# Twelve chunks of windowed attention and a two-layer network on one core: both halves of layer 1 by Strassen from the seventh chunk on, layer 2 in two banks, LayerNorm's squares on ScalarE

## The chip, the core and the metric

The kernel runs on one core of a Trainium2 chip. The core has five engines that run side by side, each through its own list of instructions in order: TensorE (PE; matrix products into the eight banks of PSUM; loads of its weights are listed as PEld), VectorE (DVE), ScalarE (ACT), GpSimd (POOL) and SyncE (SP; it issues DMAs). They wait for each other by semaphores. The metric is the time of one execution on the device in microseconds (us), as the median over runs.

## What is computed

Attention of 4 batches, 8 heads, 768 tokens, head size 64, over a window of 128 tokens and 4 sink tokens; then LayerNorm and a two-layer network of 512, 2048 and 512, and a residual:

```python
scores = scale * np.matmul(q, k.transpose(0, 1, 3, 2))
is_sink = pos[None, :] < n_sink                   # 4
in_window = (rel >= 0) & (rel < window)           # 128
a = softmax(np.where(is_sink | in_window, scores, -1e9))
x = np.matmul(a, v)                               # heads side by side: 4 x 768 x 512
xn = (x - mean(x)) / np.sqrt(var(x) + 1e-06) * g_ln
out = x + np.maximum(xn @ w_ch1, 0.0) @ w_ch2
```

Inputs and output are float32. Inside, operands of matrix products are bfloat16 and sums are float32.

## The kernel before

The 3072 tokens are cut into 24 tiles of 128 (t) and 12 chunks of 256 (c = 0 to 11, three to a batch; R = c % 3). A chunk goes through these steps, named by the operations in the program:

- **Loads.** GpSimd's queue loads q and k (`nat`, 128 KB a tile) and v (`vn`), casting to bfloat16. From chunk 4 on SyncE's queue transposes q and k by DMA into `kq` (`trq`, `trk`). Chunks 0 to 3 are transposed on TensorE (L672 for chunks 1 to 3, from `n4a`, `n4b`, `n4c`).
- **Attention.** `sc` (L754, L802): scores on TensorE into a pair of PSUM banks; `ex` (L758, L814): exponentials on ScalarE; `mk` (L826; a quarter of it on GpSimd, L821): masks on VectorE; `sv` (L721) and `av` (L854): values on TensorE, with the sum of the weights as a 65th column of every head.
- **LayerNorm.** On VectorE `rc` (reciprocal, L868), `x` (L870), `bn` (BN_STATS, L874) and `ag` (L876); on GpSimd `rs` (L882, L883: 1/sqrt of the variance); on VectorE `xc` (L885: centred and scaled). From chunk 2 on SyncE's queue transposes `xc` into `xnt` by DMA (L569), two transposes a chunk.
- **Layer 1.** Plain units `ph` (L1027): 8 matmuls of 256 columns into one bank, clipped into the hidden tile `hq` by ScalarE or VectorE (`rl`, L1037, L1039). From chunk 4 on the first half of the hidden columns (`hq[0]`) is made by Strassen's seven products `m1` to `m7` (L958, 8 matmuls of 128 columns each), with token sums `xt` on GpSimd (L938) and weight sums made once on VectorE (`wsum`, L923). Three product banks z, w, y are used; `tz` (L969) are copies of a bank to SBUF on ScalarE, after which the next product adds to the same bank; the sums `c11`, `c12`, `c22` are VectorE additions of a bank and a copy (L980) followed by a clip on ScalarE (L983); `c21` is clipped from its bank (L1001). The other half stays with four units.
- **Layer 2.** From chunk 2 on seven products `p1` to `p7` (Winograd's form, L1109, 8 matmuls of 256 columns each) with VectorE's operand sums `s1` to `s4` (L1092), the keeping sums `tm` (L1123: bank plus x) and the final sums `o` (L1130); the order is p1, p2, p7, p6, p4, p5, p3 in three banks x, y, w. SyncE's queue stores the result (L1154, L1159).

The order of all this is not that of the text. `Plan.op` only records operations with their engines, reads, writes and a priority; `Plan.run` then simulates the engines with a table of costs, gives each operation an engine, a start and its buffers out of the rings (`nat`, `kq`, `hq`, `tz`, the PSUM banks `one` and `pair`), and the operations are emitted in the order of these starts. Into TensorE's gaps of that simulated time before 24 us the last loop of the program lays matmuls on a tile of zeros (`junk`, L1236).

## Time and profile before

| what | value |
|---|---|
| time, median of 3 runs | 208.83 us (208.38 to 208.92) |
| span of the profiled execution | 206.6 us; it is an execution of its own, and its whole time is not listed apart |
| ScalarE, GpSimd busy, 140 to 155 us | 9.22 and 8.46 of 15 us |
| software DMA queue (GpSimd's) | 13.37 MB, 81.7% of 16 engines' span |
| hardware DMA queue (SyncE's) | 13.43 MB, 34.1% |
| median time from issue to landing, k, q, v | 4.6, 4.9, 6.9 us |

The span runs from the first to the last instruction; the time also holds what lies before and after it. A busy time adds up an engine's instructions, and two that overlap are counted twice. In the chain of waits each piece is followed back from the last instruction to what released it, so that its shares say what the end hangs on.

### The profile page before, as it was taken

What the parts mean: (1) busy time and instruction counts of PE and PEld (TensorE: products, weight loads), DVE (VectorE), ACT (ScalarE), POOL (GpSimd) and SP (SyncE); (2) the same over time, 40 slices, a digit from 0 to 9 for tenths busy, and PEclk for the clock granted to TensorE, in tenths of its full rate; (3) what the DMA queues carried; (4) which work ended last, traced back from release to release, by engine and by line L of the source; (5) the groups of instructions that cost most, each with busy time, mean ns of one, the idle gap of its engine ahead of it and who ended that gap; (6) DMA issues with size and microseconds to landing.
All of it is one profiled execution on the core that took longest, in us unless ns stands there. A gap on an engine that the chain in (4) does not pass through costs nothing.

```text
span 206.6 us, 6790 instructions
## 1 busy us (share of the span) xinstructions
PE 199.4 (97%) x2766; PEld 165.6 (80%) x2766; DVE 179.6 (87%) x437; ACT 119.7 (58%) x187; POOL 118.7 (57%) x170
## 2 busy tenths in 40 slices
PE   6888999999999999999999999999999999999994
PEld 2557996674698897898998988988988988988993
DVE  7589769899599899899989989989989989998693
ACT  3649477839555655666486486485486585560620
POOL 7977475279039029959649949968627229125000
PEclk9999999999999999999999999999999999999999
DMA  5999999999999999999999999899976411210302
GB/s 117 146 195 195 197 181 205 199 158 171 186 200 124 124 191 101 121 174 101 175 152 137 113 159 143 109 171 114 194 117 101 128 33 23 106 32 19 108 27 84
DMA packets 101341, 27.55 MB, mean 133 GB/s; under 512 B 89652, under 2 KB 99128, under 8 KB 101304
## 3 DMA queue, kind: packets, MB, share of 16 engines
q0 software_dynamic: 67712, 13.37, 81.7%
q1 hardware_dynamic: 33304, 13.43, 34.1%
q8 instruction: 22, 0.36, 0.7%
q10 hardware_dynamic: 288, 0.26, 0.4%
q14 instruction: 15, 0.12, 0.2%
HBM read 27.31 MB, written 6.29 MB: 163 GB/s over the span
## 4 chain that ended last, share of the span: by engine, by line
PE 90%; DMA 3%; DVE 3%; POOL 2%; issue 0%; DVEq 0%
PE one L1109 31%; PE one L1027 20%; PE one L958 12%; PE one L1058 7%; PE one L1020 7%; PE pair L854 5%; PE pair L802 4%; DMA n4b<-in_q_dram 3%; PE one L672 1%; PE pair L721 1%; POOL nat L626 1%; PE one L714 1%; DVE xnt L907 1%; DVE kq L595 1%; POOL vn L589 0%; DVE st L874 0%
## 5 line engine op out<-in xcount | busy, mean ns | idle before, releaser
L1027 PE MATMUL one<-xnt,w 128*128 128x256 bf16 x384 | 46.8, 273 | 0.0
L814 ACT ACTIVATE pe<-pair 128x1024 bf16<-128x1024 f32 (+1 forms) x40 | 36.3, 963 | 18.2 <-PE pair L802 18.2
L1037 ACT ACTIVATE hq<-one 128x512 bf16<-128x512 f32 x58 | 33.4, 590 | 17.9 <-PE one L1020 9.4
L1027 PEld LDWEIGHTS <-w 128*128 128x128 bf16 x384 | 36.3, 98 | 4.0
L1109 PEld LDWEIGHTS <-hs 128*128 128x128 bf16 x320 | 31.0, 98 | 4.0
L882 POOL TENSOR_SCALAR st<-st 128x1 f32<-128x1 f32 x24 | 6.4, 266 | 44.4 <-DVE rec L868 27.5
L826 DVE TENSOR_TENSOR pe<-pe,mask 128x1024 bf16<-128x1024 bf16 (+1 forms) x35 | 27.1, 799 | 1.6 <-ACT pe L814 1.4
L969 ACT COPY tz<-one 128x512 f32<-128x512 f32 x24 | 13.9, 585 | 20.6 <-PE one L958 19.2
L1109 PEld LDWEIGHTS <-hq 128*128 128x128 bf16 x240 | 22.2, 98 | 4.1 <-issue 0.5
L589 POOL DMA_DIRECT2D vn<-in_v_dram x24 | 21.9, 922 | 2.2 <-DMA w<-in_moe_w_ch_dram 1.2
L983 ACT ACTIVATE hq<-hq 128x512 bf16<-128x512 bf16 x24 | 15.1, 630 | 13.1 <-DVE hq L980 12.6
L1109 PE MATMUL one<-w,hq 128*128 128x256 bf16 x160 | 19.2, 273 | 0.0
L980 DVE TENSOR_TENSOR hq<-one,tz 128x512 bf16<-128x512 f32 x24 | 16.4, 684 | 1.9 <-PE one L958 1.0
L1130 DVE TENSOR_TENSOR ot<-one,tm 128x256 f32<-128x256 f32 x40 | 15.9, 412 | 2.1 <-PE one L1109 1.8
L1123 DVE TENSOR_TENSOR tm<-one,x 128x256 f32<-128x256 f32 x40 | 16.6, 414 | 1.2 <-PE one L1109 1.1
L870 DVE TENSOR_TENSOR x<-pair,rec 128x512 bf16<-128x512 f32 x24 | 16.6, 691 | 0.8
L874 DVE BATCH_NORM_STATS2 st<-x 128x6 f32<-128x512 bf16 x24 | 16.5, 687 | 0.2
L1020 PE MATMUL one<-xnt,w 128*128 128x128 bf16 x256 | 16.0, 219 | 0.5 <-DVE xnt L907 0.5
L687 POOL DMA_DIRECT2D nat<-in_q_dram x16 | 14.2, 893 | 3.7 <-DMA w<-in_moe_w_ch_dram 3.7
L938 POOL TENSOR_TENSOR xt<-xnt 128x256 bf16<-128x256 bf16 x16 | 12.2, 778 | 7.1 <-DMA xnt<-xc 7.0
L687 POOL DMA_DIRECT2D nat<-in_k_dram x16 | 14.8, 928 | 2.4 <-DMA w<-in_moe_w_ch_dram 2.4
L1020 PEld LDWEIGHTS <-w 128*128 128x128 bf16 x256 | 14.6, 98 | 1.6 <-issue 0.8
(130 smaller groups left out, 387.7 us busy)
## 6 DMA issues: line engine op xcount, KB each, us to landing
out_dram<-ot SPq DMA_DIRECT2D x17, 256.0 KB
w<-in_moe_w_ch_dram POOLq DMA_DIRECT2D x8, 512.0 KB, 12.8
vn<-in_v_dram POOLq DMA_DIRECT2D x24, 128.0 KB, 6.9
nat<-in_k_dram POOLq DMA_DIRECT2D x17, 128.0 KB, 4.6
nat<-in_q_dram POOLq DMA_DIRECT2D x17, 128.0 KB, 4.9
out_dram<-ot SPq DMA_DIRECT2D x14, 128.0 KB
kq<-nat SPq DMA_TRANSPOSE x32
xnt<-xc SPq DMA_TRANSPOSE x20
```

The costliest lines, as they stand in the source:

```text
L589: loads[b * RB + r, "v"] = P.op(f"vld{t}", {"POOL": (0.87, 0.9)}, prio, lambda e: G.dma_start(bv.t[:, :, 0:64], v[b, :, 128 * r:128 * (r + ...
L687: lambda e, nat=nat, ap=ap: G.dma_start(nat.t, ap), writes=[nat], dma=SW if c < 6 else (*SW[:2], PAR["llag"]), after=behind(c, 0 if soon e ...
L814: P.op(f"ex{c}{hp}", {"ACT": act(2 * n)}, d + 0.1 + 0.05 * j, lambda e, pp=pp, pb=pb: nc.scalar.activation(pb.t[:, :, 0:n], pp.t[:, :, 0:n ...
L826: V.tensor_mul(pb.t[:, :, 0:n], pb.t[:, :, 0:n], mm),
L870: P.op(f"x{t}", {"DVE": dve(512)}, d + xo + 0.11, lambda e: V.tensor_tensor(x.t.rearrange("p (a h c) -> p a h c", a=2, c=64), pv()[:, :, : ...
L874: P.op(f"bn{t}", {"DVE": fix(0.60)}, d + xo + 0.12, lambda e: V.bn_stats(st.t[:, 8:14], x.t), reads=[x], writes=[st, mv])
L958: nc.tensor.matmul(b.t[:, 128 * h:128 * h + 128], lhsT=lt[:, kk, 128 * h:128 * h + 128], rhs=rh[:, kk, :], start=first and h == 0 and kk = ...
L1020: nc.tensor.matmul(ph.t[:, 128 * s:128 * s + 128], lhsT=w1[u // 2][:, j, 128 * s:128 * s + 128], rhs=xnt.t[:, j, 128 * (u % 2):128 * (u % ...
L1027: nc.tensor.matmul(ph.t[:, 256 * s:256 * s + 256], lhsT=w1[ht // 4][:, j, 128 * (ht % 4):128 * (ht % 4 + 1)], rhs=xnt.t[:, j, :], start=j ...
L1037: nc.scalar.activation(hg.t[:, u % 4, :], ph.t, AF.Relu)
L1109: nc.tensor.matmul(at(r), lhsT=get(left, g)[:, v, s, :], rhs=rhs, start=first and n == 0, stop=n == 7, skip_group_check=True)
L1123: return P.op(f"tm{name}_{c}", {"DVE": dve(256, 1.14)}, pr - PAR["kp"], lambda e: V.tensor_tensor(tm[name].t, at(r), xs[i].t[:, sl], op=AL ...
```

## The change

In words:

- The simulated planner goes. `SCHEDULE` is a table with an engine and a start for each of the 1159 operations, `SLOTS` one with the buffer of each; `run` reads them. The order of chunks 0 to 3 stays as it was, apart from the fills on `junk`, which follow the table's gaps.
- The ring `one` has, beside its four banks, the four halves of the `pair` banks; `tz` has three tiles in place of two.
- From chunk 6 (`new=6`) `both()` makes both halves of the hidden columns by Strassen: 14 half products and no units. The sums are one VectorE instruction each that adds and clips (`TENSOR_ADD_SAT`). From chunk 7 the copy of m1 goes from bank to bank (`sd`, ScalarE), m2 adds to it, and c11 is a clip. A second set of weight sums (`wsumb`) is made on VectorE in chunks 4 to 6.
- From chunk 6 layer 2 goes p1, p2, p6, p7, p5, p4, p3 and alternates between two banks.
- From chunk 7 (`lnc=7`) `x` is made by an instruction that also sums the row, followed by a small scaling (`nm`); the squares are summed by ScalarE (`sq`); `rs` has a third step; `xc` is made by VectorE or ScalarE; the token sums by VectorE or GpSimd. The values lie 128 columns apart in the bank instead of 65.

The core of the diff:

```diff
+    def run(self):
+        engines = dict(P="PE", A="ACT", V="DVE", G="POOL", S="SP")
+        table = SCHEDULE.split()
+        assert len(table) == len(self.ops)
+        for o, entry in zip(self.ops, table):
+            o.eng, o.start = engines[entry[0]], int(entry[1:]) / 100
...
+        return sorted(self.ops, key=lambda o: (o.start, o.seq))
...
-    P.ring("one", [Slot(ones[i], f"one{i}", [banks[4 + i]]) for i in range(4)])
+    P.ring("one", [Slot(ones[i], f"one{i}", [banks[4 + i]]) for i in range(4)]
+           + [Slot(pairs[i][:, j, :], f"half{i}{j}", [banks[2 * i + j]], 1, True) for i in range(2) for j in range(2)])
...
-    ring("tz", 2, [128, 512], FP32)
+    ring("tz", 3, [128, 512], FP32)
...
+            P.op(f"x{t}", {"DVE": fix(0.62)}, d + xo + 0.11, lambda e: V.tensor_tensor_reduce(
+                out=x.t.rearrange("p (h c) -> p h c", c=64), in0=pv()[:, :, 0:64],
+                in1=rc().unsqueeze(2).to_broadcast([128, 8, 64]), scale=1.0, scalar=0.0, op0=ALU.mult, op1=ALU.add,
+                accum_out=st.t[:, 13:14]), reads=[po, rcb], writes=[x, st])
+            nm = Buf(f"nm{t}")
+            P.op(f"nm{t}", {"DVE": fix(0.07)}, d + xo + 0.12, lambda e: V.tensor_scalar_mul(
+                st.t[:, 12:13], st.t[:, 13:14], -1.0 / DM), reads=[st, x], writes=[nm])
+            P.op(f"sq{t}", {"ACT": (0.78, 0.9)}, d + xo + 0.13, lambda e: nc.scalar.activation(
+                xc.t, x.t, AF.Square, bias=st.t[:, 12:13], accum_out=st.t[:, 15:16]), reads=[x, st, nm], writes=[mv, xc])
...
+            G.tensor_tensor(st.t[:, 16:17], st.t[:, 17:18], mhalf, op=ALU.pow),
+            *([G.tensor_tensor(st.t[:, 8:9], st.t[:, 16:17], st.t[:, 12:13], op=ALU.mult)] if on_act else [])),
...
+            P.op(f"xc{t}", {"DVE": fix(0.33), "ACT": act(512)}, d + xo + 0.6, lambda e: V.tensor_scalar(
+                xc.t, x.t, st.t[:, 12:13], st.t[:, 16:17], op0=ALU.add, op1=ALU.mult) if e == "DVE" else nc.scalar.activation(
+                xc.t, x.t, AF.Identity, bias=st.t[:, 8:9], scale=st.t[:, 16:17]), reads=[x, st, mv, rs], rw=[xc])
...
+    def both(c, T, g, hq, tokens):
...
+        def total(n, bank, done, tz, pr):
+            outs[n] = Buf(f"{n}_{c}{g}")
+            o = P.op(f"c{n}_{c}{g}", {"DVE": dve(512, 1.14)}, pr, lambda e: V._custom_dve(
+                dve_ops.TENSOR_ADD_SAT, out=block(n), in0=banks_[bank].t.rearrange("p (i t) -> p i t", i=4),
+                in1=tz.t.rearrange("p (i t) -> p i t", i=4), s0=FMAX, s1=0.0),
+                reads=[done, tz], hold=[banks_[bank], hq], writes=[outs[n]])
+            return o
...
+        m1 = product(1, "z", "a11", "b11", True, second[:1])
+        if seeds:
+            seed = Buf(f"sd{c}{g}")
+            o1 = P.op(f"sd_{c}{g}", {"ACT": act(512)}, T + pos[0] - PAR["tzp"], lambda e: nc.scalar.copy(banks_["w"].t, banks_["z"].t),
+                      reads=[m1], hold=[banks_["z"]], writes=[banks_["w"], seed])
+        else:
+            t1, o1 = snap(1, "z", m1)
+        m5 = product(5, "y", 0, "t0", True)
+        t5, o5 = snap(5, "y", m5)
+        m2 = product(2, "w", "a12", "b21", not seeds, [o1] if seeds else [])
...
+        m6 = product(6, "z", 1, "t1", False, [o1])
+        t2, o2 = snap(6, "z", m6)
+        m3 = product(3, "y", 3, "b22", False, [o5])
+        total("c12", "y", m3, t2, T + pos[5] - late_)
+        m7 = product(7, "z", 2, "t2", False, [o2])
+        o3 = total("c22", "z", m7, t5, T + pos[6] - late_)
+        m4 = product(4, "z", "a22", "t3", False, [o3])
...
-        quick = halves(c, T, hq[0]) if strassen else None
-        for u in range(4 if strassen else 0, NH1 // 2):
+        tokens = token_sums(c, T) if strassen else None
+        quick = ([both(c, T, g, hq[g], tokens) for g in range(2)] if c >= PAR["new"] else [halves(c, T, hq[0], tokens)] if strassen else [])
+        for u in range(4 * len(quick), NH1 // 2):
...
+            bank = {n: Buf(f"bk{n}{c}", "one", full=True) for n in "xy"}
+            reg = {"z": ("x", 0), "l2": ("y", 256), "l1": ("y", 0), "r1": ("x", 256)}
```

What the table moves, at the three places that matter below.

TensorE between the last scores of tile 1 (`pair_62<-kq_85`) and chunk 1's transposes (`n4b`), before and then changed:

```order
L742 LDWEIGHTS ident
L742 MATMUL pair_62<-neg,ident 128x512
...
L754 LDWEIGHTS kq_85
L754 MATMUL pair_62<-kq_85 128x128
...
L672 LDWEIGHTS n4b_68
L672 MATMUL one_64<-ident,n4b_68 64x2x64
```

```order
L741 LDWEIGHTS kq_85
L741 MATMUL pair_62<-kq_85 128x128
...
L1351 LDWEIGHTS junk
L1351 MATMUL one_65<-junk 128x512
...
L1351 LDWEIGHTS junk
L1351 MATMUL one_65<-junk 128x128
...
L658 LDWEIGHTS n4b_68
L658 MATMUL one_64<-ident,n4b_68 64x2x64
```

Eight matmuls on the tile of zeros, six of 512 columns and two of 128, now stand ahead of the 32 transposes.

ScalarE in layer 1 of chunk 8 (`tz`: copies of a bank; `hq`: clips; `pe`: exponentials; in the changed kernel `one<-one` is the copy from bank to bank, `xc,st<-x` the squares and `xc<-x` the centred tile), before and then changed:

```order
L969 COPY tz_146<-one_66 128x512
L969 COPY tz_147<-one_63 128x512
L983 ACTIVATE hq_131<-hq_131 128x4x128
L1037 ACTIVATE hq_132<-one_64 128x512
L969 COPY tz_146<-one_66 128x512
L983 ACTIVATE hq_131<-hq_131 128x4x128
L1037 ACTIVATE hq_132<-one_65 128x512
L983 ACTIVATE hq_131<-hq_131 128x4x128
L1037 ACTIVATE hq_132<-one_64 128x512
L1037 ACTIVATE hq_132<-one_63 128x512
L1001 ACTIVATE hq_131<-one_66 128x4x128
```

```order
L1075 COPY one_65<-one_66 128x512
L1069 ACTIVATE hq_129<-one_65 128x4x128
L867 ACTIVATE xc_119,st_159<-x_106,st_159 128x512
L1075 COPY one_65<-pair_62 128x512
L1049 COPY tz_146<-pair_62 128x512
L1049 COPY tz_148<-one_66 128x512
L1049 COPY tz_147<-pair_62 128x512
L867 ACTIVATE xc_120,st_164<-x_107,st_164 128x512
L1049 COPY tz_147<-pair_61 128x512
L1069 ACTIVATE hq_130<-one_65 128x4x128
L1069 ACTIVATE hq_130<-pair_62 128x4x128
L1069 ACTIVATE hq_129<-one_66 128x4x128
```

The copies go from three to six, the clips of sums and of units are gone, and LayerNorm's squares stand between the copies.

VectorE in the LayerNorm of one chunk (`st`: statistics of a tile), before and then changed; ISA rows are the new instructions, the one of 128x1 reads the row sum out:

```order
L868 RECIPROCAL rec<-pair_62 128x8
L870 TENSOR_TENSOR x_111<-pair_62,rec 128x512
L980 TENSOR_TENSOR hq_131<-one_65,tz_146 128x4x128
L874 BN_STATS st_159<-x_111 128x6
L876 BN_AGGR st_159<-st_159 128x2
L868 RECIPROCAL rec<-pair_61 128x8
L870 TENSOR_TENSOR x_110<-pair_61,rec 128x512
```

```order
L859 RECIPROCAL rec<-pair_62 128x8
L860 ISA x_106,st_159<-pair_62,rec 128x512
L860 ISA st_159 128x1
L859 RECIPROCAL rec<-pair_61 128x8
L865 TENSOR_SCALAR st_159<-st_159 128x1
L860 ISA x_107,st_164<-pair_61,rec 128x512
L860 ISA st_164 128x1
```

The statistics pass over the tile is gone from VectorE; a read-out and a small scaling take its place.

418 lines of the change are left out of this document (238 added, 180 removed).

## The prediction

> **What bounds the kernel now.** I read the page first, then the chain of waits in order of time, then the busy time by stretches of about one chunk.
>
> ```profile
> span 206.6 us, 6790 instructions
> PE 199.4 (97%) x2766; PEld 165.6 (80%) x2766; DVE 179.6 (87%) x437; ACT 119.7 (58%) x187; POOL 118.7 (57%) x170
> PE 90%; DMA 3%; DVE 3%; POOL 2%; issue 0%; DVEq 0%
> ```
>
> TensorE is busy for 97% of the span and makes 90% of the chain that ended last. Where the other 10% lie is seen in the chain's early pieces (start, length, what):
>
> ```profile
> 5.50 7.09 DMA n4b<-in_q_dram
> ...
> 12.73 0.65 PE one L672 x16
> 13.41 1.23 DVE kq L595
> ...
> 18.01 0.70 DVE xnt L907
> ...
> 18.75 1.05 PE one L1020 x16
> ```
>
> Until 12.6 us the chain is a load of q; then 16 transposes, then VectorE without a pause to 18.71, then TensorE to the last product. So before 18.75 a late transpose is a late VectorE, and whatever is late at 18.75 is late at the end. After it only TensorE counts. In the stretches (TensorE, weight loads, VectorE, ScalarE, GpSimd busy; clock; DMA) this is plain:
>
> ```profile
> 124.00:140.00 16.00, 16.00 (x225) 14.13 (x222) 14.99 (x38) 10.73 (x18) 13.64 (x19) 1.00 1.23 139
> 171.00:187.00 16.00, 16.00 (x218) 14.13 (x216) 15.55 (x37) 8.46 (x15) 6.04 (x10) 1.00 0.18 52
> ```
>
> TensorE has no idle time at full clock. VectorE looks nearly as full, but its busy times overlap: rows of 0.41 us follow each other every 0.33 to 0.34 us in the last fence of this text, so about 0.07 us of each of the 38 rows is counted twice, and 14.99 of 16 us is nearer 12.3.
>
> **The change part by part.**
>
> *Matrix work.* Chunks 6 to 11 replace four plain 512-wide units of layer 1 by seven half products. One period of the chain prices both:
>
> ```profile
> 132.07 0.89 PE one L958 x16
> 132.96 0.87 PE one L1027 x8
> ...
> 136.53 1.75 PE one L1027 x16
> ```
>
> A unit is 8 matmuls of 256 columns, 0.873 us; a half product is 8 of 128 columns, 0.445. Four units are 3.49, seven half products 3.12: 0.377 a chunk, and for six chunks **-2.26 us**, all of it on the path. Layer 2 keeps seven products of the same size.
>
> *The start.* The planner is replaced by a table, and the fill matmuls on junk, laid into the gaps that the table shows, change with it: eight new ones (six of 512 columns, two of 128) stand between the last score matmuls of tile 1 (L754) and chunk 1's transposes (L672). TensorE there:
>
> ```profile
> 10.45 0.92 PE L1236 MATMUL one<-junk 128*128 128x512 bf16 x5
> 11.21 0.59 PE L742 MATMUL pair<-neg,ident 128*128 128x512 bf16 x2
> 11.73 0.40 PE L754 MATMUL pair<-kq 64*128 64x128 bf16 x8
> 12.73 1.08 PE L672 MATMUL one<-ident,n4b 128*64 128x128 bf16 x32 [0.60 <-DMA n4b<-in_q_dram]
> ```
>
> The five old fills (1792 columns) hold the engine for 11.21 - 10.45 = 0.76 us, so the eight new ones (3328 columns) take 1.41. They begin when L754 is issued, at 12.06 to 12.13, and end at 13.47 to 13.54; the transposes were ready at 12.73. The idle 0.60 is cover for less than half of the fills. Behind the transposes stands VectorE's copy at 13.41 and its unbroken run to 18.71, so the delay reaches the end: 0.74 to 0.81, **+0.78**.
>
> *Tighter loops between TensorE and the evicting engines.* A Strassen product into a bank that is read before the next product adds to it makes a loop: product issued, copy (ScalarE) or sum (VectorE), next product.
>
> ```profile
> 130.65 0.61 PE L958 MATMUL one<-xnt,w 128*128 128x128 bf16 x8
> ...
> 131.35 0.59 ACT L969 COPY tz<-one 128x512 f32<-128x512 f32 x1 [1.44 <-PE one L958]
> ...
> 137.93 1.06 ACT L1037 ACTIVATE hq<-one 128x512 bf16<-128x512 f32 x2
> ...
> 139.09 0.99 PEld L1109 LDWEIGHTS <-hq 128*128 128x128 bf16 x10 [0.16 <-ACT hq L1037]
> ```
>
> The sum's row in the groups of instructions (line, operation, count | busy us, mean ns | idle before):
>
> ```profile
> L980 DVE TENSOR_TENSOR hq<-one,tz 128x512 bf16<-128x512 f32 x24 | 16.4, 684 | 1.9 <-PE one L958 1.0 <-ACT tz L969 0.4
> ```
>
> The product's issue ends at 130.65 + 0.445 = 131.10, the copy starts 0.25 later and takes 0.59; the weight load that waits for ScalarE's two clips starts 0.10 after their end at 138.99. So a copy needs 0.94 us of other matrix work, a sum 0.25 + 0.68 + 0.10 = 1.03. In the kernel before, plain units (0.87) stand between the half products and no loop is short. In the changed order I count six copies and three sums in chunks 7 to 11 with only 0.89 between (two half products, or one and a score group): short by 0.05 six times and by 0.14 three times, 0.72 in all. Several of these overlap, so that one wait covers the next: I take **+0.5**; it can be 0.2, or 1.0 if an eviction queues behind an exponential.
>
> The sum that also clips is a new VectorE instruction. Its nearest row is L980's 0.684 (same sources, shape and output); the upper end is that plus ScalarE's pass that it replaces, 0.63 (L983 below). I take 0.68, since each element is still read once.
>
> *LayerNorm from chunk 7.* The groups that carry it:
>
> ```profile
> L882 POOL TENSOR_SCALAR st<-st 128x1 f32<-128x1 f32 x24 | 6.4, 266 | 44.4 <-DVE rec L868 27.5
> ...
> L874 DVE BATCH_NORM_STATS2 st<-x 128x6 f32<-128x512 bf16 x24 | 16.5, 687 | 0.2
> ...
> L983 ACT ACTIVATE hq<-hq 128x512 bf16<-128x512 bf16 x24 | 15.1, 630 | 13.1 <-DVE hq L980 12.6
> ...
> L883 POOL TENSOR_TENSOR st<-st,mhalf 128x1 f32<-128x1 f32 x24 | 14.6, 608 | 2.0
> ...
> L876 DVE BATCH_NORM_AGGREGATE st<-st 128x2 f32<-128x6 f32 x24 | 4.3, 179 | 0.5
> ```
>
> Per tile the chain loses 0.69 + 0.18 and gains a read of the sum and a small scaling on VectorE (0.18 each, as L876), the squares on ScalarE (0.63, as L983) and a third small GpSimd step (0.27 to 0.61): longer by 0.4 to 0.7, less than nothing only if the new steps cost half of their rows. VectorE's load per chunk: -1.73 for the two tiles' statistics, +0.72 for the small steps, +0.68 for one more sum, and about three token sums moved over from GpSimd at up to 0.42: +0.9 on 12.3 of some 15.3 us. It is no bound, and ScalarE, which loses three clip passes and four unit evictions and gains copies and squares, stays near 60%. Both are hidden behind TensorE, except in the loop that this chain closes: values out of TensorE, LayerNorm, two DMA transposes, first half product. The timeline has it (the last row is the view by tile: shortest, median and longest issue in ns):
>
> ```profile
> 133.67 0.65 PE L854 MATMUL pair<-vn,pe 128*128 128x65 bf16 x16
> ...
> 137.81 3.24 SPq L569 DMA_TRANSPOSE xnt<-xc  x2
> ...
> 144.93 1.65 POOL L938 TENSOR_TENSOR xt<-xnt 128x256 bf16<-128x256 bf16 x2 [1.08 <-DMA xnt<-xc]
> ...
> 152.43 2.51 SPq L569 DMA_TRANSPOSE xnt<-xc  x2
> ...
> 157.48 1.48 POOL L938 TENSOR_TENSOR xt<-xnt 128x256 bf16<-128x256 bf16 x2 [0.92 <-DMA xnt<-xc]
> ...
> 183.15 2.59 SPq L569 DMA_TRANSPOSE xnt<-xc  x2
> ...
> 187.13 1.48 POOL L938 TENSOR_TENSOR xt<-xnt 128x256 bf16<-128x256 bf16 x2 [3.06 <-DMA xnt<-xc]
> L569 SPq DMA_TRANSPOSE xnt<-xc x17: 1189/1192/1999, 62.8 to 184.6; - x17
> ```
>
> One transpose is issued in 1.19 us, so the second ones start at 139.86, 153.75 and 184.55 and have landed 5.07, 3.73 and 2.58 later: with six loads in flight, with transposes of the next chunk behind them, and with neither. In chunk 8 the values' issue ends at 133.67 + 0.48 = 134.15, the loop closes at 144.93: 10.78 us. With the new LayerNorm that is 11.2 to 11.5, or 9.8 to 10.1 at the landing of 3.73. The changed order has between them, in chunk 8, 14 half products, 4 layer 2 products and 2 score groups of 0.44: 10.6 us. The loads of q, k and v are issued one or two at a time there instead of four and six, so I take a landing half-way (4.4): 10.7 on average, **+0.1**; the ends are 0 and 0.9 for this chunk.
>
> [...]
>
> *Layer 2 and the end.* Two products instead of three lie between the first one and its follower; the keeping sum of 0.41 needs 0.25 + 0.41 + 0.10 = 0.76 of the 0.87 between, so nothing waits. At the end chunk 10's last products now stand among chunk 11's:
>
> ```profile
> 184.07 6.38 PE one L1109 x56
> ...
> 198.68 0.41 DVE L1092 TENSOR_TENSOR hs<-hs,hq 128x512 bf16<-128x512 bf16 x1
> 199.02 0.41 DVE L1123 TENSOR_TENSOR tm<-one,x 128x256 f32<-128x256 f32 x1
> 199.35 0.41 DVE L1092 TENSOR_TENSOR hs<-hs,hq 128x512 bf16<-128x512 bf16 x1
> ```
>
> Seven products are 6.11 us, so chunk 10 waited 0.27 for its sums, which the mixing can save; against it about 26 VectorE steps at 0.34 now stand beside 10 products (8.7 us), a tie. I count zero, with 0.3 either way. The tail behind the last product is the same sum and store.
>
> Sum: -2.26 + 0.78 + 0.5 + 0.1 = -0.88. The profiled execution's span is 206.6; 2.2 us lie between it and the median of 208.83, and the change touches nothing there. So 205.7 for the span, **207.95** for the time.
>
> **The rivals.**
> 1. *The start's delay does not arrive.* For it: TensorE has many short queues later. Against: no idle time after 18.75 in which to catch up. Then -1.66: 207.2.
> 2. *The LayerNorm loop sets the pace* (slower). Place: the first half product of a chunk waits for the second transpose of xc. It decides as soon as landing stays at 5.07: 0.6 to 0.9 in chunk 8, and where little work stands between, in chunks 10 and 11 (9.56 and 9.25 us), 0 to 0.8 each at 3.73; scores can wait in the same way for kq, whose transposes now wait for later loads. Some 2.0 in all: -0.98 + 2.0 = +1.0, 209.85. Against: loads are thinner there.
> 3. *Evictions come 0.1 later* than the rows say on the two dozen loops that have 0.1 to 0.2 to spare: +0.9 more, 208.8. For it: ScalarE has longer passes in the same queue.
> 4. *The clipping sum costs two passes,* 1.31: 0.6 too much on some five close loops, +3: 211.
>
> **How the numbers follow.** Forecast 0.45 (its own range 207.4 to 208.6), rival 1 0.15, 2 0.22, 3 0.13, 4 0.05. Time: 208.0. Range 206.9 to 209.9: rival 4, the upper third of 2 and a little of 1 fall out, under 0.2. Within 0.3% (0.63 us, about what a measurement here tells from no change) is 208.2 to 209.46. Faster: two thirds of the forecast and rival 1, 0.44. Same: the rest of the forecast, most of 3, some of 2, 0.31. Slower: most of 2, 4 and a little of 3, 0.25.
>
> **What will show it.** Right: a full row of eight fills ahead of the first transposes of n4b, these at about 13.5 and not 12.73, and L1020's second group at about 19.5 instead of 18.75; seven half products in place of four units from chunk 6; TensorE idle in pieces of 0.05 to 0.2 released by copies and sums; the new sum at 0.68. Wrong: TensorE waiting for xnt or kq by half a microsecond (rival 2), the new sum above 0.8 (rival 4), or transposes at 12.7 (rival 1).

## The result

The changed kernel takes 215.25 us (median of 4 runs, 214.77 to 215.73) against 208.61 for the kernel before (4 runs, 208.23 to 208.92). The ratio is 1.031, with a 95% interval of 1.029 to 1.034: slower by 6.6 us, where 0.8 less was forecast. The span of the profiled execution goes from 206.6 to 213.3. Executions more than 1.5% above the fastest of their kernel are left out of the times and ratios below; the traces of loads, mended and stacked are of such executions and show where those lost time, not what the quicker ones lost.

The page of the changed kernel, lines as shown of before:

```profile
span 213.3 us, 7116 instructions
PE 201.5 (94%) x2916; PEld 167.1 (78%) x2916; DVE 178.8 (84%) x460; ACT 125.6 (59%) x203; POOL 107.3 (50%) x165
PE 26%; ACT 5%; DMA 4%; POOL 3%; DVE 3%; issue 2%; SPq 1%; ACTq 0%; POOLq 0%; DVEq 0%
```

The changed kernel's chain can be followed back only to 117.0 us, so its shares cover 44% of the span, and TensorE's 26 of these 44 are 60% of that piece, where it had 90% of the whole span before: the chain now leaves TensorE again and again. Its busy time cannot tell how much was lost, since a stalled matmul's modelled end reaches into the gap. So I take the times between the issues of neighbouring matmuls, less the columns they stream (some 2.4 per ns: 512 take 0.216 us); differences of 0.11 us and less (about 0.095 each, most of them where matmuls of one tile shape follow another, here called switches) are kept apart. Stalls worked out in this way, in us:

| | 24-109 | 109-127 | 127-140 | 140-156 | 156-171 | 171-187 | 187-last product | sum |
|---|---|---|---|---|---|---|---|---|
| before | 0.18 | 0 | 0 | 0 | 0 | 0.12 | 0.13 | 0.43 |
| changed | 0.16 | 1.46 | 1.03 | 1.94 | 0.53 | 0.51 | 1.02 | 6.65 |

The last product is issued at 203.14 before and at 207.87 now, 4.73 later: the matrix work gives -2.26, the start +1.11 in this execution, the stalls +6.22, fewer switches some -0.3. Behind the last product come 3.45 us before and 5.42 now, +1.97. That is the whole of 6.7 us to within 0.1.

Who ends TensorE's idle time from 24 to 212 us (engine, tile and line, releaser: us in total, times, longest):

```profile
PE pair L1038 <- DVE hq L1060: 1.4, 3, 0.6
PE pair L1038 <- ACT tz L1049: 1.0, 4, 0.3
PE one L1206 <- DVE tm L1220: 0.6, 1, 0.6
PE one L1038 <- DMA xnt<-xc: 0.3, 1, 0.3
PE pair L707 <- ACT pe L801: 0.3, 1, 0.3
```

These are 3.6 us, less than the stalls of issue because of the modelled ends, but they show the places. Half products (L1038) into halves of `pair` wait 2.4 us for sums and copies; those into the four banks `one` only 0.3, for transposes. The timeline of the second half of chunk 8 (TensorE, then ScalarE, then VectorE) shows what such a wait is:

```profile
150.05 0.61 PE L1038 MATMUL one<-xt,hq 128*128 128x128 bf16 x8
150.99 0.61 PE L1038 MATMUL pair<-xt,hq 128*128 128x128 bf16 x8 [0.32 <-ACT tz L1049]
151.43 0.61 PE L1038 MATMUL one<-xnt,w 128*128 128x128 bf16 x8
152.26 0.61 PE L1038 MATMUL pair<-xnt,hq 128*128 128x128 bf16 x8 [0.23 <-ACT tz L1049]
152.71 0.61 PE L1038 MATMUL one<-xt,hq 128*128 128x128 bf16 x8
153.76 0.61 PE L1038 MATMUL pair<-xt,hq 128*128 128x128 bf16 x8 [0.45 <-DVE hq L1060]
```

```profile
150.34 0.59 ACT L1049 COPY tz<-pair 128x512 f32<-128x512 f32 x1
150.82 0.60 ACT L1049 COPY tz<-one 128x512 f32<-128x512 f32 x1
151.63 0.58 ACT L1049 COPY tz<-pair 128x512 f32<-128x512 f32 x1 [0.20 <-PE pair L1038]
```

```profile
153.02 0.69 DVE L1060 CUSTOM_DVE_ANT_0 hq<-pair,tz 128x512 bf16<-128x512 f32 x1 [1.40 <-ACT xc L867]
```

The product at 150.05 is issued by 150.50, the next one only at 150.99: 0.49 lost, then 0.39 and 0.61. Banks z and y of this half of the hidden columns lie in the two halves of one `pair` tile (half10 and half11). The copy that ended at 150.93 is that of y, and it releases m6, which writes z; the copy that ended at 152.21 is that of z, and it releases m3, which writes y; m7 into z waits for the sum out of y. `SLOTS` places the halves as banks of their own, but the waits of the program hold for the tile as a whole.

VectorE and ScalarE, stretches as in the prediction and two more (TensorE, weight loads, VectorE, ScalarE, GpSimd; clock; DMA), then one of these two in the kernel before, and the new instructions' groups:

```profile
109.00:125.00 16.00, 15.04 (x251) 13.16 (x248) 15.13 (x35) 9.41 (x17) 12.42 (x17) 1.00 1.68 141
124.00:140.00 16.00, 15.42 (x261) 13.59 (x259) 13.64 (x37) 11.79 (x22) 10.05 (x19) 1.00 1.26 115
140.00:156.00 16.00, 14.87 (x221) 13.39 (x219) 13.48 (x37) 10.45 (x19) 11.15 (x17) 1.00 1.44 138
171.00:187.00 16.00, 15.65 (x281) 14.22 (x278) 12.31 (x33) 12.98 (x23) 3.47 (x8) 1.00 0.57 55
```

```profile
109.00:125.00 16.00, 16.00 (x244) 14.13 (x243) 14.75 (x35) 10.36 (x17) 12.67 (x17) 1.00 1.19 133
```

```profile
L1060 DVE CUSTOM_DVE_ANT_0 hq<-pair,tz 128x512 bf16<-128x512 f32 x13 | 8.8, 687 | 7.4 <-PE pair L1038 5.9 <-ACT xc L867 1.4
L867 ACT ACTIVATE xc<-x,st 128x512 bf16<-128x512 bf16 x10 | 7.2, 720 | 7.0 <-DVE st L865 6.7
L867 ACT ACTIVATION_READ_ACCUMULATOR xc<-x,st 128x1 f32 x10 | 1.9, 187 | 0.0
L889 ACT ACTIVATE xc<-x,st 128x512 bf16<-128x512 bf16 x5 | 4.1, 816 | 1.1 <-POOL st L885 1.1
L885 POOL TENSOR_TENSOR st<-st 128x1 f32<-128x1 f32 x10 | 2.1, 211 | 0.8
```

The sum that clips costs 0.69, as the plain sum did before. The squares cost 0.72 + 0.19 on ScalarE, a centred tile made there 0.82; that is 0.09 and 0.19 more than the clip of before (0.63).

The end: the flag that every engine reads before its last branch (by the tile `flag`, and by the line of ScalarE's last branch; of before, then changed; line, queue, operation: ns, first and last start):

```profile
L1202 DVE CAST flag<-one x1: 147/147/147, 190.6 to 190.6; 1x1 int32<-1x1 f32 x1
```

```profile
L1240 ACTq COMPARE_BRANCH  x1: 50/50/50, 197.9 to 197.9; - x1
L1240 ACTq EVENT_SEMAPHORE  x1: 17/17/17, 200.4 to 200.4; - x1
```

```profile
L1317 DVE CAST flag<-pair x1: 146/146/146, 208.2 to 208.2; 1x1 int32<-1x1 f32 x1
```

```profile
L1355 ACTq COMPARE_BRANCH  x1: 50/50/50, 208.9 to 208.9; - x1
L1355 ACTq EVENT_SEMAPHORE  x1: 17/17/17, 211.8 to 211.8; - x1
```

The table makes the flag's product stand among chunk 11's last ones, and the flag is written 17.6 us later than before. ScalarE's first instruction behind its branch comes 2.5 to 2.9 us after it; that used to lie beside TensorE's work and now ends at 211.8. The last store, issued at 209.14, is seen as landed at 212.34 (3.2 us; before 203.90 and 205.63, 1.7). So in this execution the end hangs on the store and not on the flag: the store is issued 1.26 us behind the last product (0.76 before) and lands 1.5 us more slowly, and these two make the 1.97.

### The profile page after: what moved, and what is told of

The parts are those of the page before. It is cut to its first block, busy times and chain, and to the rows that moved or that the text cites. A ratio compares the mean times of both kernels' runs of the same rounds, so it can differ in the third digit from the quotient of the medians.

```text
span 213.3 us, 7116 instructions
## 1 busy us (share of the span) xinstructions
PE 201.5 (94%) x2916; PEld 167.1 (78%) x2916; DVE 178.8 (84%) x460; ACT 125.6 (59%) x203; POOL 107.3 (50%) x165
## 5 line engine op out<-in xcount | busy, mean ns | idle before, releaser
L1131 ACT ACTIVATE hq<-one 128x512 bf16<-128x512 f32 x30 | 17.9, 598 | 18.6 <-PE one L1113 9.4
L1038 PEld LDWEIGHTS <-hq 128*128 128x128 bf16 x384 | 23.2, 98 | 3.1 <-issue 2.6
L1206 PEld LDWEIGHTS <-hq 128*128 128x128 bf16 x240 | 22.7, 98 | 3.5 <-issue 0.7
L813 DVE TENSOR_TENSOR pe<-pe,mask 128x1024 bf16<-128x1024 bf16 (+1 forms) x35 | 23.5, 689 | 2.1 <-ACT pe L801 1.9
L1038 PEld LDWEIGHTS <-w 128*128 128x128 bf16 x288 | 17.8, 98 | 2.2 <-issue 1.1
L1121 PE MATMUL one<-xnt,w 128*128 128x256 bf16 x144 | 17.4, 273 | 0.0
L1185 DVE TENSOR_TENSOR hs<-hq 128x512 bf16<-128x512 bf16 x40 | 16.0, 418 | 1.3 <-ACT hq L1069 1.0
L1220 DVE TENSOR_TENSOR tm<-one,x 128x256 f32<-128x256 f32 x36 | 15.0, 418 | 1.9 <-PE one L1206 1.7
L884 POOL TENSOR_TENSOR st<-st,mhalf 128x1 f32<-128x1 f32 x24 | 14.7, 611 | 2.0
L1227 DVE TENSOR_TENSOR ot<-one,tm 128x256 f32<-128x256 f32 x36 | 14.7, 417 | 0.9 <-DMA out_dram<-ot 0.6
L1152 PE MATMUL one<-w,hq 128*128 128x512 bf16 x64 | 15.0, 380 | 0.0
L1060 DVE CUSTOM_DVE_ANT_0 hq<-pair,tz 128x512 bf16<-128x512 f32 x13 | 8.8, 687 | 7.4 <-PE pair L1038 5.9
```

What stands on the lines that cost most here:

```text
L813: V.tensor_mul(pb.t[:, :, 0:n], pb.t[:, :, 0:n], mm),
L884: G.tensor_tensor(st.t[:, 16:17], st.t[:, 17:18], mhalf, op=ALU.pow),
L1038: nc.tensor.matmul(b.t[:, 128 * h:128 * h + 128], lhsT=lt[:, kk, 128 * h:128 * h + 128], rhs=rh[:, kk, :], start=first and h == 0 and kk = ...
L1121: nc.tensor.matmul(ph.t[:, 256 * s:256 * s + 256], lhsT=w1[ht // 4][:, j, 128 * (ht % 4):128 * (ht % 4 + 1)], rhs=xnt.t[:, j, :], start=s ...
L1131: nc.scalar.activation(hg.t[:, u % 4, :], ph.t, AF.Relu)
L1152: nc.tensor.matmul(pc.t[:, 0:wd], lhsT=(hq[s // 2].t[:, (2 * s + i) % 4, 128 * ii:128 * ii + 128] if by_tile else hq[ht // 8].t[:, ht // 2 ...
```

## The experiments

Starts in `SCHEDULE` only set the order, so most edits are two small dictionaries: `MOVE` gives an operation another start, `PLACE` a buffer another slot, by

```diff
-            o.eng, o.start = engines[entry[0]], int(entry[1:]) / 100
+            o.eng, o.start = engines[entry[0]], MOVE.get(o.name, int(entry[1:]) / 100)
...
-            b.slot = self.rings[b.ring][int(n, 36)]
+            b.slot = self.rings[b.ring][PLACE.get(b.name, int(n, 36))]
```

Ratios are to the kernel before, run beside each; the changed kernel's own is 1.031 (1.029 to 1.034), and again 1.029 (1.024 to 1.034). A lead is how much earlier than in the changed kernel's profile TensorE issues the same product.

**The start.** The fills ahead of chunk 1's transposes go.

```diff
-        if free and left > 0.11:
+        if free and left > 0.11 and o.name != "tr10":
```

> The changed kernel without the eight matmuls on zeros between the scores of tile 1 and the transposes of chunk 1. Theory of the prediction's second term, now from the trace of the changed kernel: the fills end at 13.8 us, the q load lands at about 12.75, and the delay is carried to the end: 1.0 to 1.1 us less than 215.25, so about 214.2; the first group of 32 transposes starts at 12.7 to 12.8 in place of 13.84. Rival (the delay is caught up later or was made earlier, by the slow clock of the first fills): 215.0 to 215.3.

214.73 us, 1.030 (1.025 to 1.034): nothing that the times can tell. In the profile TensorE is 1.05 ahead until 144 us and 0.28 at the last product. Nor are the 1.05 the fills' alone: two kernels with all of them (pair_order and lock6, below) reached this place as early. In 14 profiled executions that hold these fills the second group of plain units of chunk 1 starts between 18.64 and 20.04, on average at 19.42; in the five without them between 18.56 and 19.25, on average at 18.85. So the fills delay by about 0.56 on average. Much of the spread comes from further ahead, as one row of the start shows in the changed kernel's first and second execution:

```profile
4.07 1.91 PE L729 MATMUL pair<-neg,ident 128*128 128x512 bf16 x4
```

```profile
4.07 1.24 PE L729 MATMUL pair<-neg,ident 128*128 128x512 bf16 x4
```

TensorE starts at half its rate, with 0.43 us for 512 columns, and later needs 0.22. By the clock records of the traces it goes over at 7.2 us in the first execution and at 4.5 in the second, and between 4.5 and 7.7 in all 20. The first transposes (L635) start at 5.69 to 6.84 us, right behind the matmul ahead of them, and never earlier where the clock goes over later.

**The changed kernel again**, as base for three later runs.

> The changed kernel unchanged, as the base for the other three on the same chip: 214.8 to 217, ratio 1.028 to 1.036. Every theory expects the same.

215.04 us, 1.029. Its profiled execution starts 0.56 ahead of the first one and is 0.13 ahead at the last product. So a lead that no edit made is lost too, by stalls of 7.00 instead of 6.65 in all.

**LayerNorm as before** (statistics on VectorE in all chunks, in the same places of the table; `new` and the rest as changed).

```diff
-PAR = dict(lnc=7,
+PAR = dict(lnc=12,
```

> The changed kernel with LayerNorm as it was before the change (statistics by VectorE, two GpSimd steps, the centred tile by VectorE) in the same places of the order. Rival theory (the new LayerNorm on ScalarE and GpSimd makes the idle time of 124 to 176 us): 2 us or more less, 213 or below. Theory of banks and of VectorE's and GpSimd's queues: only the idle pieces that end with a centred tile or squares on ScalarE go (0.47 at 131 and 0.38 at 169 us), and VectorE gets 1.5 us more work a chunk: 214.5 to 216.

217.19 us, 1.040 (1.037 to 1.043): undoing the new LayerNorm wins nothing; without it the same table is 1.9 us slower, with stalls of 9.2.

**VectorE's second weight sums** (this leaves out seven eighths of their columns, so the output of the later chunks is not the reference's).

```diff
-V.tensor_tensor(ap(), val(x0), val(x1), op=op)
+V.tensor_tensor(*((ap(), val(x0), val(x1)) if not g else (z[:, 0:1, 0:128] for z in (ap(), val(x0), val(x1)))), op=op)
```

> The four sums of weights for the second half (L931, made on VectorE in chunks 4 to 6) are cut to 128 of their 1024 columns, so that this work is nearly gone; the products read the rest as it lies in the buffer. If VectorE is the engine that lacks time in chunk 6 (it was busy 109 to 117 us without a gap, and TensorE stalled 0.20 + 0.75 + 0.51 us from 113.3 to 117.7), these 1.46 us go: TensorE is 1.2 to 1.5 ahead at chunk 7 and, if the lead stays, the time is 213.8. If the pace there is set by the pairing of the halves or by transfers, under 0.4 is gained by chunk 7. If leads are lost again later, as with the start, the lead at chunk 7 is there and the time is 214.5 to 215.2.

215.01 us, 1.027 (1.020 to 1.033). The stalls of 0.95 were gone and TensorE 1.5 ahead (0.56 of it from the start) when a single stall of 1.94 took it all, at 117.6. It waited for a sum of VectorE, which stood behind this (VectorE, then GpSimd):

```profile
113.55 0.41 DVE L1220 TENSOR_TENSOR tm<-one,x 128x256 f32<-128x256 f32 x1
113.89 2.73 DVE L1185 TENSOR_TENSOR hs<-hq,hs 128x512 bf16<-128x512 bf16 x1
116.54 0.41 DVE L1220 TENSOR_TENSOR tm<-one,x 128x256 f32<-128x256 f32 x1
```

```profile
113.83 0.69 POOL L946 TENSOR_TENSOR xt<-xnt 128x256 bf16<-128x256 bf16 x1
114.46 1.24 POOL L808 TENSOR_SCALAR_AFFINE_SELECT pe<-pe 128x512 bf16<-128x512 bf16 x2
115.66 0.66 POOL L946 TENSOR_TENSOR xt<-xnt,xt 128x256 bf16<-128x256 bf16 x1
```

A pass that takes 0.41 elsewhere starts 0.06 after GpSimd's first of four passes without a gap, and ends at 116.62, 0.3 after the last of them ended.

**That hold by itself.** lock6 changes the order of two of GpSimd's instructions in chunk 6, so that a load's issue stands ahead of its masks; tiny_pool cuts GpSimd's passes to 8 columns from chunk 6 on; mask7 gives GpSimd's mask of chunk 7 to VectorE and makes the last weight sum later.

```diff
+MOVE = {'xtt2_6': 113.2, 'vld17': 114.0}
```

> In chunk 6 GpSimd issues a load of v between its token sums and its masks, and not between its first two and its third token sum, so that VectorE's mask finds GpSimd at a DMA issue. If GpSimd's passes hold VectorE, the mask (1.15 in the changed kernel) takes 0.55 to 0.7 and the stall of 0.75 at 116.3 falls by 0.4 to 0.75. If VectorE is only full, the mask stays and the stall is 0.6 to 0.8.

217.39 us, 1.040 (1.034 to 1.045): slower by over 2 us, by two instructions that changed places.

```profile
114.27 2.84 DVE L814 TENSOR_TENSOR pe<-pe,mask 128x1024 bf16<-128x1024 bf16 x1
117.03 0.41 DVE L1221 TENSOR_TENSOR tm<-one,x 128x256 f32<-128x256 f32 x1
```

```profile
113.74 0.92 POOL L576 DMA_DIRECT2D vn<-in_v_dram  x1
114.67 1.25 POOL L809 TENSOR_SCALAR_AFFINE_SELECT pe<-pe 128x512 bf16<-128x512 bf16 x2
115.88 0.67 POOL L947 TENSOR_TENSOR xt<-xnt,xt 128x256 bf16<-128x256 bf16 x1
```

The mask (0.68 elsewhere) waited through three passes and ended 0.55 after them; TensorE's stall of 0.75 became 2.44. Its row even begins 0.4 ahead of the first of them, during the load's issue. The hold is shown; the expectation that a load's issue would let the mask through was wrong.

The stall is not all of the loss. Behind it TensorE ran at half its clock (columns as in the stretches above; lock6, then mask7, the last run of this part):

```profile
118.00:121.40 3.40, 3.40 (x26) 2.86 (x25) 2.75 (x6) 0.00 (x0) 0.00 (x0) 0.50 0.67 177
```

```profile
118.00:121.40 3.40, 3.40 (x69) 3.08 (x67) 3.40 (x7) 0.22 (x1) 0.77 (x1) 1.00 0.61 158
```

The granted clock is 0.50 in place of 1.00 and 26 matmuls are issued in place of 69; the differences too small for a stall add up to 8.1 us in this run and to 6.5 in the changed kernel. Such a stretch of 3.4 us stands in five runs, in or soon after one of their longest stalls (2.44 here, 2.45 in stacked, 3.13 in mended, 3.12 in light_loads, 2.10 in loads); a stall of 1.94 (small_sums) and the other long one of loads (2.13) had none behind them, and what brings it no run shows. In these five runs the small differences come to 1.2 to 2.0 us more than in the changed kernel, beside the stall itself.

```diff
+                            m = (4, 128) if c < 6 else (1, 8)
+                            v = v[:, 0:m[0], 0:m[1]]
...
-                right(n), right(x0), right(x1), op=ALU.subtract)
+                *(z[:, 0:1, 0:8] for z in (right(n), right(x0), right(x1))), op=ALU.subtract)
```

> GpSimd's passes over tensors are cut to 8 columns from chunk 6 on: the token sums (L946) and its quarter of the masks (L808); chunk 6's token sums use the other buffer. If VectorE's bf16 passes are held up while GpSimd passes over a tensor (a pass of 0.42 took 2.73 us in the run before this, ending with the fourth of GpSimd's passes that followed each other without a gap), then from chunk 6 on no mask (L813) takes over 0.6 and no sum of weights (L931) over 0.72, the stalls at 113.3 and 116.3 (0.95) and at 117.7 (0.51) are gone and TensorE is 1.2 to 1.5 ahead at chunk 7; the time is 213.0 to 214.2 if half of it stays. If VectorE is only too full, the passes stay as they were and under 0.4 is gained by chunk 7.

The cut masks leave weights in the sums that the program's guard does not accept, so its second, general path runs behind the first: 1256 us, and only the trace up to there counts. The stalls at 113 and 116 (0.95 in the changed kernel) are gone; 0.61 at 109.5 and 0.74 at 117.8 stand in their place.

```diff
+MOVE = {'mk70': 116.8, 'wsumb2': 119.4}
...
-                if R and c > PAR["half"] and hp in PAR["mkp"]:
+                if R and c > PAR["half"] and c != 7 and hp in PAR["mkp"]:
```

> Chunk 7's first mask goes from GpSimd to VectorE (behind the final sums of chunk 5), and the last of the second weight sums is made 6.6 us later, so that GpSimd has no run of passes left while VectorE makes its masks in chunk 6; VectorE's work until 118 us is about the same. If GpSimd's passes hold VectorE, no VectorE pass takes over 1.2 us, the stall of 0.75 at 116.3 falls under 0.3, and the time is 0.3 to 0.9 below the changed kernel's (ratio to before 1.025 to 1.028). If VectorE is only full, the stall stays at 0.6 to 0.9 and the time within 0.3.

215.13 us, 1.030 (1.026 to 1.035): within 0.3 of the base. No pass takes over 1.2, the stall of 0.75 at 116.3 is gone, and TensorE, 0.74 ahead there, is level with the base at chunk 8: 0.75 of wait for the sum in the other half at 117.2 (0.51 in the base), then 0.6 in three pieces.

**The halves of `pair`.** banks moves y and z of chunks 7 and 8 (here two w banks are overwritten where they should be added to, so the output of these chunks is another one); pair_order keeps the computation.

```diff
+PLACE = {'mz7_0': 1, 'mw7_0': 4, 'my7_1': 6, 'my7_0': 5, 'mz8_1': 2, 'my8_1': 6, 'mw8_1': 4, 'my8_0': 7}
```

> The changed kernel, order as it was, with other PSUM banks for layer 1 in chunks 7 and 8, so that the two halves of a pair tile are no longer both used by products that alternate (z and y of chunk 8's second half leave the same tile). Theory: the built waits treat the two halves of a pair tile as one, so a product waits for the copy or sum of the other half; in chunk 8 that costs 0.49 + 0.39 + 0.61 and in chunk 7 0.43: 1.5 to 1.9 less, 213.3 to 213.8, and the three idle pieces before the products of 150 to 154 us go. Rival (the copies and sums are simply too slow for the new order, whatever the bank): 215.0 to 215.5 and the idle pieces stay.

213.80 us, 1.026 (1.019 to 1.032). The three stalls of chunk 8, 1.49, were gone; that of chunk 7, 0.43, became 0.73; and 1.25 were lost at 156.75: scores waited 1.1 for the transposes of k and q, which were no earlier.

```diff
+MOVE = {'cc11_60': 115.92, 'cc12_111': 192.98}
+PLACE = {'my8_1': 4}
```

> Two sums are emitted behind the product of the other half that waited for them (cc11 of chunk 6 behind m3, cc12 of chunk 11 behind m4), and chunk 8's y bank of the second half moves to the other pair. If the waits come from two halves of one pair tile, the stalls of 0.51 (117.7), 1.49 (151 to 153.8) and 0.77 (198.5) fall to 0.5 or less in all. If the gain is kept the time is 2.0 to 2.7 below the changed kernel's; if VectorE and the transfers take it back as in the earlier runs, 0.3 to 1.2 below.

214.97 us, 1.031 (1.022 to 1.039), in two groups, 213.28 and 213.76, 216.18 and 216.20. In the profiled execution, 213.76, the wait of chunk 8 falls from 1.49 to 0.24 and that of chunk 11 from 0.77 to 0.18, as expected; but 1.00 is lost at 156.2 (transposes of q and k) and 0.90 behind 197.8 (VectorE's sums of layer 2). TensorE is 1.22 ahead at chunk 1, where no edit lies, 2.07 past chunk 8 and 1.20 at the last product: what the edits won is gone.

**Transfers.** loads puts four loads of v behind the GpSimd step they delayed, one q load into another buffer, and a store ahead of two transposes. light_loads brings one head of eight in chunks 8 to 11 (their output is not the reference's).

```diff
+MOVE = {'vld19': 122.5, 'vld16': 122.55, 'vld22': 165.3, 'vld23': 165.35, 'st140': 152.9}
+PLACE = {'qn100': 5}
```

> Transfers alone: the four v loads that stand ahead of rs in GpSimd's queue (chunks 8 and 10) go behind it, chunk 10's q load goes to another nat buffer, and chunk 7's store goes ahead of a pair of transposes on SP. If the stalls at 131.4 (0.47, exponentials behind xc behind rs behind loads), 169.1 to 169.7 (0.54, sum behind a late store) and 175.5 (0.51, xnt behind rs) are queues' and add up: -1.5, 213.7. If each lead is lost at the next stall: 214.5 to 215.2.

216.40 us (215.88 and 216.91; two more took 219.90 and 220.75), 1.035 (1.026 to 1.043): not better, and far more spread. The loads now run beside the transposes of xc (chain, start, length):

```profile
139.81 6.20 DMA xnt<-xc
146.06 0.62 PE one L1040 x8
```

6.2 us from issue to landing, and TensorE waits 2.1 for it, and 2.1 again at 178.4 for a later one. Of the three stalls aimed at, only that of 169 went.

```diff
-            bv.t[:, :, 0:64], v[b, :, 128 * r:128 * (r + 1), :].rearrange("h p d -> p h d")),
+            *((bv.t[:, 0:n, 0:64], v[b, 0:n, 128 * r:128 * (r + 1), :].rearrange("h p d -> p h d")) for n in (8 if t < 16 else 1,)).__next__()),
...
-G.dma_start(nat.t, ap)
+G.dma_start(*((nat.t, ap) if c < 8 else (nat.t[:, 0:1, :], ap[:, 0:1, :])))
```

> The loads of q, k and v for chunks 8 to 11 bring one head of eight, so that the DMA engines are nearly free from about 110 us on; everything else is as in the changed kernel. If the landing of the transposes of xc and of q and k sets chunks 8 to 11, they land 2.5 to 3.0 us after their issue, no wait for xnt or kq is left on TensorE, and the stalls 131.4, 141.1, 169.1 and 175.5 (1.6 in all) go: 213.5 to 214.3. If the transfers only take up slack: 214.8 to 215.3.

216.89 us, 1.038 (1.032 to 1.045). Of the four stalls named, those at 131.4 and 169.1 went and that at 175.5 fell to 0.32; the two pieces at 141 stayed (0.21 and 0.25), so they are no wait for a transfer. An operand sum of layer 2 on VectorE (0.41 elsewhere) took 3.15 beside GpSimd's passes, TensorE waited 3.12 at 115.6 and fell into the half clock; of the 3.2 us it was behind then, 2.1 were left at the last product.

**The end.** flag_early gives the flag's product its early place, end_order puts chunk 11's layer 2 in the old order, stores finishes chunk 10 first (there a kept sum of chunk 10 is overwritten before its use, so a quarter of that output is another one).

```diff
+MOVE = {'guard': 181.6, 'gsum': 183.25, 'gflag': 183.6}
+PLACE = {'ptf': 6}
```

> The changed kernel with the check of the reciprocals (guard, its sum on TensorE, its flag on VectorE) moved from the very end to 181.6, 183.3 and 183.6 in the table. Theory: all engines read the flag before they may finish; the flag is written at 208.2, behind the last product, so ScalarE, GpSimd and SyncE read it late and the span ends 4.6 us after the last sum in place of 2.7: 1.9 us less, 213.3. Rival (the tail is the landing of the last stores, which wait for nothing of the flag): 215.0 to 215.4.

214.77 us, 1.027 (1.024 to 1.031). ScalarE branches at 201.4, and the tail is 4.89 instead of 5.42 us. That is within the scatter: in the 13 profiled executions with the late flag it is 5.00 to 6.08 (6.05 in the unchanged kernel's second), in the four with the early one 4.89, 5.47, 5.86 and 6.28. So the flag is not shown to be worth anything. TensorE also lost 1.75 at 159.3 to transposes of q and k, which this edit does not touch.

```diff
+MOVE = {'p7_11': 196.92, 'p6_11': 198.67, 'p4_11': 199.54, 'p5_11': 200.42, 'p3_11': 201.36,
...
```

> Chunk 11's layer 2 alone in the order p1, p2, p7, p6, p4, p5, p3, so that its four stores of 128 KB are issued one product (0.87 us) apart and not three of them within 1.6 us. If these three stores behind the last product make the tail 5.1 us, it falls to 3.3 to 4.0 and the time by 1.1 to 1.8: 213.4 to 214.2. If the tail is set by something else, it stays: 214.8 to 215.5.

216.91 us, 1.037 (1.031 to 1.044). The last stores are issued 0.8 to 2 us apart, and the tail stays at 5.6; the last store still takes 3.1 to land, and the flag is still late: ScalarE branches at 211.3 and goes on at 214.3, as late as the store. So this run does not tell what either costs alone; VectorE, given its sums in another order, cost 2.1 us of stalls besides.

```diff
+MOVE = {'p5_10': 194.29, 'p4_10': 195.16, 'p2_11': 196.04, 'p3_10': 196.92, 'p6_11': 197.79,
...
```

> The end alone: chunk 10's last three products of layer 2 stand ahead of chunk 11's, so that its two stores of 256 KB are issued some 2 us earlier. If these stores make the tail behind the last product 5.1 instead of 3.2 us, the tail falls to 3.4 to 4.0 and the time by 1.0 to 1.7, to 213.6 to 214.2. If the flag or the last store itself makes it, the tail stays at 4.6 to 5.1 and the time at 214.8 to 215.3.

216.24 us, 1.032 (1.025 to 1.039): the tail does not fall (6.1 us).

**All together.** mended joins no_fills, flag_early, loads, stores and the order of two sums (and has the overwritten sum of stores); light_all joins no_fills, tiny_pool, light_loads and chunk 7's and 8's y banks (cut masks and loads, so again the second path); stacked joins no_fills, flag_early, pair_order and lock6; stacked2 the same with mask7 in place of lock6.

> All at once: no fills ahead of chunk 1's transposes, the flag early, chunk 7's and 8's y banks in the pair of the other half's y and not of its z (my7_0 and my8_1 to half01 and half00), the loads, the end, and two sums placed behind the product that only waits for them because they share a pair of banks. If the loss is the sum of these waits, each with its own cause (start 1.1, banks 1.5, loads 1.5, end and flag 1.5, two sums 1.2), up to 6.8 comes back: 208.5 to 210.5, about the time of the kernel before. If the leads are lost again to VectorE and to transfers that cannot come earlier, 212 to 213.5.

219.52 us, 1.050 (1.041 to 1.059). A mask took 3.68 beside GpSimd's passes, TensorE waited 3.13 for it, with the half clock behind, and twice 1.8 to 2.0 for transposes of xc.

> Both cuts together, with no fills ahead of chunk 1's transposes and the y banks of chunks 7 and 8 in the pair of the other half's y. If what took each earlier lead away was GpSimd's hold on VectorE and the DMA engines, the leads now stay and add up: 1.1 from the start, 1.4 from chunk 6, 1.5 from the banks, 1.6 from the transfers, 5.6 in all, 209.6 to 211. If VectorE's own work or the loop from the values to the next chunk's products takes them away again: 213 to 214.5.

Only the trace up to the second path counts. The last product comes 1.95 earlier than in the changed kernel. A lead of 0.6 from the start was gone by 27 us, to a wait for weights that no edit touches, so the 1.95 are the edits' and were kept. Stalls are 6.1, 1.7 of them ahead of 60 us. In the waits of TensorE 2.1 us are those of half products in `pair` for sums, and 0.5 for xnt; none is for a mask or for the transposes of q and k.

> Both, with no fills ahead of chunk 1's transposes and the flag made early. If the lost time is a sum of independent waits: 1.1 + 2.5 + 0.6 + 0.5 = 4.7 below the changed kernel's time, 210.5 to 212. If leads are taken back by whatever comes next: 0.5 to 2 below, 213 to 215.

215.79 us, 1.034 (1.028 to 1.040), with lock6's mask of 2.84 and its half clock.

> That with no fills ahead of chunk 1's transposes, the flag early, the two sums behind the products of the other half and chunk 8's y bank in the other pair. If the lost time is a sum of waits with causes of their own, now that VectorE's hold is out of the way: 1.1 + 0.7 + 2.3 + 0.5 = 4.6 below the changed kernel's, 210.3 to 211.5 (ratio 1.007 to 1.013). If transfers and VectorE still take a part back: 212 to 213.8 (ratio 1.015 to 1.024). If all is taken back again: 214.5 and more.

214.63 us, 1.027 (1.024 to 1.031): the lowest median of those that leave nothing out, but 4.6 were hoped for and some 0.5 came. TensorE's idle time from 24 to 212 us in it:

```profile
PE one L1041 <- DMA xnt<-xc: 0.6, 1, 0.6
PE pair L846 <- DVE pe L816: 0.5, 2, 0.3
PE one L1209 <- DVE hq L1063: 0.3, 1, 0.3
PE pair L710 <- ACT pe L804: 0.3, 1, 0.3
PE pair L1041 <- ACT tz L1052: 0.3, 1, 0.3
PE one L1041 <- DVE ot L1230: 0.2, 1, 0.2
```

The waits in `pair` are down from 2.4 to 0.3; masks, sums and transposes have taken their place, and the stalls of issue are 6.94 in all. It was 1.0 ahead at 60 us, 2.2 past chunk 6 (117.7) and 0.9 at the last product.

## Why the prediction was wrong

Forecast was a gain of 0.88, measured a loss of 6.6 us. Two terms failed above all: the loops between TensorE and the evicting engines, put at +0.5, and the tail, put at 0. The stalls are 6.22 us more than before, 3.2 of them waits in `pair`, and the tail is 1.97 longer.

**Matrix work** (-2.26): right, in size too. Seven half products stand in place of four units from chunk 6. Fewer switches (some -0.3) were not counted.

**Start** (+0.78): the eight fills are there and chunk 1's transposes follow them, at 13.84 here. From the last scores to these transposes it is 1.84 us where it was 1.00 (12.00 and 11.73 to 12.73), so the term is right in this execution; the other 0.27 lay ahead of the fills. But with the same fills they came at 12.62 in another. What failed is that one execution's idle 0.60 was taken as fixed: the time at which TensorE comes to its full rate (7.2 us here) lies between 4.5 and 7.7 us in the 20 executions, and the first transposes between 5.69 and 6.84. The delay of some 0.56 on average is there, but rival 1 (it does not arrive) is what the times say: without the fills nothing was gained that can be told from noise.

**Tighter loops** (+0.5): here the prediction failed most. I counted loops between a product and the copy or sum of its own bank, 0.72 short in all, with the halves of `pair` as banks of their own, as the table has them. In the trace the long waits of that kind are for the other half: 0.51, 0.43, 1.49 and 0.77, 3.2 us in chunks 6, 7, 8 and 11. The program allocates each pair as one tile of two banks (`pairs`); I did not ask before the run what that does to the waits. Banks and pair_order show it: without the shared tile, or with the sum emitted later, the stalls of chunk 8 (in banks) and of chunks 6, 8 and 11 (in pair_order) fall to 0 to 0.24, with the same copies and sums. The two pieces at 141 (0.21 and 0.25) belong to the loops as well, for they end with sums of VectorE. Rival 4 was not it: the new sum takes 0.69. Of rival 3, the copies take 0.59 as before, and the one at 151.63 starts 0.20 behind its product's issue, where 0.25 was counted; the others' delays were not counted.

**VectorE as no bound**: wrong, and by a reading. I took 14.99 of 16 us for about 12.3, since rows overlap. The view had merged them already: the 38 rows of that stretch add up to 17.2, and 14.99 is what they cover. The busy times of the page are merged too, against what is said under the table of the profile before (VectorE's rows add up to 203.4, its busy time is 179.6). VectorE had 1 us of 16 to spare and not 4. With the second weight sums added, which I did not cost (four more rows of 0.64 to 1.16 us), it was covered for 15.13 of 16 us from 109 to 125, where TensorE lost 1.46. That a queue this full passes each delay on is argued, and it is not enough by itself: in the kernel before VectorE is covered for 14.75 us of the same stretch and 15.55 of 171 to 187, and TensorE loses 0 and 0.12 there, while the changed kernel loses 1.03 and 1.94 where VectorE is covered for 13.64 and 13.48. What the runs show is narrower: 0.95 of the 1.46 go when the second weight sums are cut or GpSimd's passes are (small_sums, tiny_pool), 0.75 when GpSimd's mask moves away and the last weight sum comes later (mask7).

**LayerNorm from chunk 7** (+0.1, and rival 2, +2.0): the third GpSimd step took 0.21 where 0.27 to 0.61 was counted, the squares 0.72 and 0.19 where 0.63 was, a centred tile made on ScalarE 0.82; undoing it all costs 1.9 us more. Of rival 2's 2.0 us of waits for xnt and kq 0.51 is seen (at 175). Another 1.0 came through queues: a load that GpSimd could not issue held back the step that xc, and then the exponentials, waited for (0.47 at 131, gone in light_loads), and a store behind transposes on SP's queue kept a final sum from its buffer (0.54 at 169, gone in loads).

**Layer 2 and the end** (0, "the same sum and store"): wrong by 1.97. The store is the same, but it is issued 0.50 later behind the last product and takes 1.5 longer to land; why, no run shows. I had not followed the flag either, a moved step that issues nothing big: its product went from 190.4 to 207.0, and ScalarE's last branch with it. ScalarE is through at 211.9, half a microsecond before the store has landed, and an early flag gave no shorter tail than the scatter.

**The sum** failed in kind as well. It set one price beside another, as if a lead on TensorE were kept. Most runs showed the opposite: what the fills, the banks, the sums or the masks won, 0.5 to 1.5 us, was mostly gone within some chunks, and so was a lead of 0.56 in the unchanged kernel. My reading is that VectorE, GpSimd's queue and the transfers had been given times by the table that TensorE could only just meet, so that a TensorE that is earlier waits longer for them; light_all, where GpSimd's passes and the loads are cut, kept its 1.95 and fits that, but no run tests it alone. In the runs with the half clock a lost lead also has that cause. What that means for the cause of the 6.6 us: the places and the releasers of the 6.2 us are shown by the trace, and that no single one of them is worth its stall is shown by the runs. Which of the joined loops would set the pace with all waits in `pair` gone and VectorE relieved at once was not tried, and stays open; so does why the last store lands later.

## What to carry to other kernels

A wait belongs to the object by which the program tracks it: before counting two banks as independent, see whether the waits know them as two (here 3.2 us were waits for the other half of a `pair`). Ask of a busy time first whether overlaps are merged (add up the rows and compare: 17.2 and 14.99 us here), for VectorE had 1 us of 16 left for the work that the change handed it, and not 4. Look for the clock behind a long stall (0.50 for 3.4 us in five runs here) before you price an edit by it. And when a whole schedule is replaced, follow the small steps as well, flags and loads, to where they end up, and price a lead by what it runs into.
